# Three quarters of the first layer of the last 1024 tokens by seven products instead of eight, with half of their squares on GpSimd

## Chip, cores and metric

One core of a Trainium2 chip. The time of a run is device microseconds from launch to end. The kernel before was timed three times: median 308.2 us (306.96, 308.2, 310.37). Lower is better.

## The reference

```python
# attention: 8 sequences, 8 heads, 576 positions, 64 wide; window of 32 to either side
scores = scale * q @ k^T;  scores = where(|i - j| <= 32, scores, -1e9)
x = softmax(scores) @ v                    # as 4608 tokens of 512
# two layers behind it: 512 -> 2048 -> 512
h = x @ w_in
r = maximum(h, 0)
out = (s * (r * r) + b) @ w_out
```

Inputs and output are float32; the kernel rounds to bf16 for its products.

## The kernel before

**Attention.** Tokens run through in units of 128 (two tiles of 64 keys). A unit has scores on TensorE (`sc<-qt,kt`, L828), an exponential on ScalarE (L856), a multiplication by a mask on VectorE (L860), the product with V on TensorE (`avn<-vb,ex`, L886) and a division on VectorE (reciprocal L908, `xn` L910). Scores of one unit and the product with V of the unit before are issued together. From the sequence PAIRS = 3 on, q and k come through GpSimd's casts (L780) and transposes by DMA (L796), and the division's result goes by a transposing DMA, issued on SyncE (L934), to `XT`, the activations with features on partitions. `XT` is a ring of 1536 tokens. V is loaded to `VST` and cast to `VB` (L605, L613 and L614).

**First layer.** `s1(m, f0)` (L1135) takes a block of up to 512 tokens and one of 16 groups of 128 features: four matmuls of 128x512 into one of two banks `W` (L1149), Relu on ScalarE into `R1` (L1156; four buffers, each for two feature groups), and once two groups are there, one square over 128x1024 on VectorE into `GT` (L1162). `GT` has two buffers, used in turn by the 512-token groups.

**Second layer.** `second(x)` (L1187) works on 512 tokens. It already uses Winograd's form of Strassen's scheme: seven products instead of eight. Each product is two chains of eight matmuls of 128x256 (L1206), so 14 such groups for 512 tokens. The sums of weights are made once (`weight_sums`, L1173), the sums of activations on VectorE (`total`, L1198: GSUM, and in place in `GT`), and VectorE combines the products with a constant and earlier products in `OUTS` (`combine`, L1222, each reads a bank `O`), which SyncE writes out (L1231). For the last group, `apart`, bank `SC` is used as well and sums S2 and S4 lie in the staging buffers 4 and 5.

**Order.** Every operation is recorded by `add` as a task with its engine, an assumed cost, the buffers that it reads and writes, and a key (the time at which it is wanted). `_Graph.plan` places the tasks one by one: of those whose inputs are there, the one that can start earliest, then the lowest key. Its assumed costs set the order alone. `emit` turns the plan into one fixed list per engine, with semaphore waits where a needed task is on another engine. Each engine then works its list in order: an instruction that waits holds up all behind it. The keys of the layers are in the tables `P1` and `P2` (L431 to L450): in a phase of 512 tokens, 16 groups of the first layer of group x and 14 of the second layer of group x - 1 are interleaved, and the second layer of the last group stands alone at the end. `due` (L471) gives the keys of attention, from the start of the block that reads its tokens.

A flag test (`flag`, L1312) near the end looks whether the exponentials stayed in range; its scratch lies in staging buffers 0 and 1.

Of the kernel before, what the change touches and what calls it, by code (L numbers as in the profile page):

```python
# [9 lines left out]
ALU = mybir.AluOpType  # L10
# [68 lines left out]
class _Graph:  # L79
# [244 lines left out]
def bass_sliding_window_symmetric__then__act_starrelu_kernel(  # L324
# [23 lines left out]
    with ExitStack() as es:  # L348
# [79 lines left out]
        def c1(m):  # L428
            return 4 * (TBLK[m][1] / 2.4 + 2.5) / 1e3
# [4 lines left out]
        for x in range(NG + 1):  # L434
            ms = BLOCKS[x] if x < NG else []
            n2 = 14 if x else 0
            work = sum(16 * c1(m) for m in ms)
            long, start = work + n2 * 0.874, at
            for m in ms:
                PH.append(at)  # L440
                share = long * 16 * c1(m) / work
                for ft in range(16):
                    P1[m, ft] = at + ft / 16.0 * share
                at += share
            for i in range(n2):
                P2[x - 1, i] = start + (i + 0.5) / n2 * long + (DELAY if x < NG else 0.0)
            at = start + long
        PH.append(P2[NG - 1, 0] - 0.5 * n2 / 14 * 0.874)
        PH.append(at)
# [113 lines left out]
        def stg_res(at, n):  # L563
            return [("STG", i) for i in range(at // 64, (at + n) // 64)]
# [251 lines left out]
        def xt_res(t0, t1):  # L816
            return [("XT", x % (XR // 32)) for x in range(t0 // 32, t1 // 32)]
# [306 lines left out]

        def place(m):

            return TBLK[m][0] // 512 % 2, TBLK[m][0] % 512

        def gt_res(gs, fc, c0, n):
            return [("GT", gs, fc, c) for c in range(c0 // 32, (c0 + n) // 32)]  # L1130

        def group(m):
            return 4 if TBLK[m][1] <= 128 else 2 if TBLK[m][1] <= 256 else 1

        def s1(m, f0):  # L1135

            t0, nt = TBLK[m]
            ng = group(m)
            wb = count["w"] % 2
            count["w"] += 1  # L1140
            both = ng == 1
            half = f0 % 2 if both else 0
# [6 lines left out]
            add("pe", [lambda e, g=g, kc=kc: e.matmul(wt[:, g, :],  # L1149
                                                      lhsT=WIN_BF[:, kc, (f0 + g) * 128:(f0 + g + 1) * 128],  # L1150
                                                      rhs=XT[:, kc, t0 % XR:t0 % XR + nt],
                                                      start=(kc == 0), stop=(kc == 3))
                       for g in range(ng) for kc in range(4)],
                1e3 * c1(m) * ng, reads=[("Win", f0 // 4, x) for x in (0, 1)] + xt_res(t0, t0 + nt),
                writes=[("W", wb)], key=key, slack=XTS)
            add("act", lambda e: e.activation(rt, wt, AF.Relu, bias=0.0, scale=1.0),  # L1156
                190 + 0.833 * ng * nt, reads=[("W", wb)], writes=[("R1", rb, half)], key=key)
# [4 lines left out]
            add("dve", lambda e: e.tensor_tensor(GT[gs][:, f1:f1 + nf, g0:g0 + nt], rr, rr, ALU.mult),  # L1162
                130 + 0.55 * nf * nt, reads=[("R1", rb, x) for x in range(2 if both else 1)],
                writes=[r for g in range(nf) for r in gt_res(gs, f1 + g, g0, nt)], key=key)

        def weights_part(y, c0):
            return WOUT_BF.rearrange("p (g y) c -> p g y c", y=2)[:, :, y, c0:c0 + HN]
# [11 lines left out]
                    reads=reads, writes=writes, key=key)  # L1179

        def g_part(x, y, t):
            return GT[x % 2].rearrange("p (g y) c -> p g y c", y=2)[:, :, y, HT * t:HT * t + HT]

        def g_res(x, y, t, halves=(0, 1)):
            return [r for h in halves for g in range(4 * h, 4 * h + 4) for r in gt_res(x % 2, 2 * g + y, HT * t, HT)]

        def second(x):  # L1187

# [54 lines left out]
                s2, s4 = (STG[i].bitcast(BF16).rearrange("p (g c) -> p g c", g=8) for i in (4, 5))  # L1243
                rs2, rs4 = (stg_res(2 * DM * i, 2 * DM) for i in (4, 5))
            for h in (0, 1):
                k = P1[max(BLOCKS[x][-1], NE), 10] if h == 0 else key[0] - 1.0
# [57 lines left out]
        for x in range(1, NG):  # L1304
            for m in BLOCKS[x]:
                attend(m)
                for ft in range(0, 16, group(m)):
                    s1(m, ft)
            second(x - 1)
        second(NG - 1)  # L1310

        def flag():  # L1312

            key = PH[-2] - 24.0
            seen = RECS.rearrange("p u h -> p (u h)")
            low, both = STG[0][:, 0:NU * H], STG[1][:, 0:NU * H]
            low_res, both_res = stg_res(0, 2 * DM), stg_res(2 * DM, 2 * DM)
# [6 lines left out]
            add("pe", lambda e: e.matmul(AVN[:, 0, 0:1], lhsT=ONESW[:, :], rhs=GOOD[:, :], start=True, stop=True), 100,  # L1324
                reads=["ONESW", "GOOD"], writes=[("AVN", 0)], key=key)
# [237 lines left out]
```

## Time and profile before

| what | value |
|---|---|
| median of three runs | 308.2 us |
| the profiled execution, whole | 309.07 us |
| its span, first to last instruction | 307.3 us |
| granted TensorE clock, mean | 1.000 |
| busy: TensorE, VectorE, ScalarE, GpSimd | 95%, 75%, 53%, 21% |
| matmuls of the first layer seen in the trace | 805 |

The profile is one execution. Group lines give line, engine, operation, destination<-sources, shape and count, then busy time in us, mean ns of one, idle time just before and who ended it. Lines in order of time give start and duration in us. PE is TensorE, DVE VectorE, ACT ScalarE, POOL GpSimd, SPq SyncE's queue of DMA issues. The modelled duration of a matmul group reaches into the next one, so the pace is read from start to start. The stretch lines give, for a window, its length and the busy time of PE, PEld (weight loads), DVE, ACT and POOL with the count of instructions, then the granted clock, the DMA share and GB/s.

### The profile page before, as it was taken

To read this page: it belongs to the slowest core of one execution; us is meant where nothing else is said; L and a number is where in the kernel's file an instruction comes from. 1 tells how busy PE (TensorE), PEld (TensorE's weight loads), DVE (VectorE), ACT (ScalarE), POOL (GpSimd) and SP (SyncE) were. 2 spreads that over 40 slices of the span, in tenths; PEclk is the share of its full clock that TensorE was granted. 3 is DMA by queue.
4 is the path that set the end of the run, shared out by engine and by line. 5 is a ranking of instruction groups with operands and counts; after the bars stand their busy time and mean duration, and the time that the engine had idled before them with its cause. 6 is when DMAs were issued, how large, how long until landed. Compare 5 with 4: busy or idle time off the path is not lost.

```text
span 307.3 us, 8802 instructions
## 1 busy us (share of the span) xinstructions
PE 292.1 (95%) x3822; PEld 211.1 (69%) x3849; DVE 230.2 (75%) x394; ACT 164.3 (53%) x261; POOL 63.3 (21%) x77
## 2 busy tenths in 40 slices
PE   8986899999999999999999999999899999999994
PEld 2455778798888887666766675666566666666784
DVE  4665798998769697977699897796876776566673
ACT  3754876695888564757465446543654433333300
POOL 5153568100000242037005400370000000000000
PEclk9999999999999999999999999999999999999999
DMA  6999999999793979999899879897803110200223
GB/s 182 316 265 319 310 288 359 285 246 229 172 194 94 246 136 163 251 236 210 158 286 200 158 178 258 191 184 141 237 17 87 53 47 22 83 30 6 69 70 107
DMA packets 118616, 54.43 MB, mean 177 GB/s; under 512 B 91232, under 2 KB 114400, under 8 KB 118576
## 3 DMA queue, kind: packets, MB, share of 16 engines
q1 hardware_dynamic: 118576, 53.85, 73.4%
q8 instruction: 31, 0.51, 0.7%
q14 instruction: 9, 0.07, 0.1%
HBM read 36.70 MB, written 9.44 MB: 150 GB/s over the span
## 4 chain that ended last, share of the span: by engine, by line
PE 78%; SPq 8%; DMA 5%; DVE 3%; issue 2%; POOL 2%; ACT 1%; POOLq 0%
PE w L1149 35%; PE o L1206 31%; DMA stg<-in_k_dram 4%; PE avn L886 4%; SPq L761 2%; PE sc L1206 2%; PE sc L828 2%; POOL nat L780 2%; SPq L796 1%; DMA vst<-in_v_dram 1%; SPq L650 1%; PE avn L917 1%; SPq L620 1%; SPq L577 1%; DVE kt L699 1%
## 5 line engine op out<-in xcount | busy, mean ns | idle before, releaser
L1149 PE MATMUL w<-xt,win 128*128 128x512 bf16 (+4 forms) x805 | 137.6, 312 | 3.8 <-issue 1.6
L1156 ACT ACTIVATE r<-w 128x512 bf16<-128x512 f32 (+2 forms) x148 | 86.2, 586 | 85.0 <-PE w L1149 82.5
L1149 PEld LDWEIGHTS w<-xt,win 128*128 128x128 bf16 x832 | 73.9, 98 | 34.9 <-ACT r L1156 1.3
L1162 DVE TENSOR_TENSOR gt<-r 128x1024 bf16<-128x1024 bf16 (+3 forms) x100 | 62.3, 629 | 31.4 <-ACT r L1156 30.9
L1206 PE MATMUL o<-wout,gt 128*128 128x256 bf16 x528 | 66.5, 273 | 0.0
L1206 PEld LDWEIGHTS o<-wout,gt 128*128 128x128 bf16 x528 | 50.9, 98 | 13.0
L780 POOL CAST nat<-stg 128x1024 bf16<-128x1024 f32 (+2 forms) x28 | 32.4, 1158 | 80.2 <-DMA stg<-in_q_dram 65.3
L856 ACT ACTIVATE ex<-sc 128x1024 bf16<-128x1024 f32 (+1 forms) x29 | 29.6, 1022 | 17.6 <-PE avn L886 16.3
L1206 PE MATMUL o<-tw,gt 128*128 128x256 bf16 x272 | 34.6, 273 | 0.0
L1222 DVE SCALAR_TENSOR_TENSOR outs<-o,sb,cvec 128x512 f32<-128x512 f32 (+1 forms) x36 | 25.7, 715 | 8.2 <-PE o L1206 7.9
L1206 PEld LDWEIGHTS o<-tw,gt 128*128 128x128 bf16 x272 | 26.3, 98 | 7.4
L1222 DVE SCALAR_TENSOR_TENSOR outs<-o,sb,outs 128x512 f32<-128x512 f32 (+1 forms) x27 | 19.3, 715 | 8.4 <-PE o L1206 8.3
L1198 DVE TENSOR_TENSOR gt<-gt 128x1024 bf16<-128x1024 bf16 (+1 forms) x26 | 23.7, 913 | 0.2
L860 DVE TENSOR_TENSOR ex<-ex,mask 128x1024 bf16<-128x1024 bf16 (+1 forms) x29 | 21.5, 740 | 1.4 <-ACT ex L856 0.9
L910 DVE TENSOR_TENSOR xn<-avn,rec 128x512 bf16<-128x512 f32 (+1 forms) x31 | 21.2, 685 | 0.5
L886 PE MATMUL avn<-vb,ex 64*64 64x65 bf16 x944 | 19.9, 197 | 0.3
L886 PEld LDWEIGHTS avn<-vb,ex 64*64 64x64 bf16 x944 | 12.9, 107 | 9.1 <-issue 4.7
L1206 PE MATMUL o<-tw,gsum 128*128 128x256 bf16 x136 | 17.6, 273 | 0.0
L1206 PEld LDWEIGHTS o<-tw,gsum 128*128 128x128 bf16 x136 | 13.1, 98 | 3.9
L1198 DVE TENSOR_TENSOR gsum<-gt 128x1024 bf16<-128x1024 bf16 x18 | 13.0, 721 | 0.4
L925 ACT COPY xt<-avn 128x512 bf16<-128x512 bf16 (+2 forms) x18 | 9.4, 531 | 4.9 <-PE avn L917 4.9
L828 PE MATMUL sc<-qt,kt 64*64 64x128 bf16 x440 | 11.7, 216 | 0.0
(132 smaller groups left out, 232.1 us busy)
## 6 DMA issues: line engine op xcount, KB each, us to landing
out_dram<-outs SPq DMA_DIRECT2D x32, 256.0 KB, 3.0
vst<-in_v_dram SPq DMA_DIRECT2D x28, 256.0 KB, 4.2
stg<-in_k_dram SPq DMA_DIRECT2D x24, 256.0 KB, 6.4
stg<-in_q_dram SPq DMA_DIRECT2D x5, 1024.0 KB, 6.5
stg<-in_moe_w_in_dram SPq DMA_DIRECT2D x8, 512.0 KB, 7.4
stg<-in_moe_w_out_dram SPq DMA_DIRECT2D x8, 512.0 KB, 7.3
stg<-in_q_dram SPq DMA_DIRECT2D x4, 512.0 KB, 8.9
stg<-in_k_dram SPq DMA_DIRECT2D x4, 512.0 KB, 8.9
```

The costliest lines, as they stand in the source:

```text
L780: (lambda e, dst=dst, src=src: e.tensor_copy(dst, src)),
L828: fns = [lambda e, pr=pr, x=x, b=b, j=j, hp=hp: e.matmul(SC[64 * x:64 * x + 64, hp, pr * 128:pr * 128 + 128], lhsT=k_tile(b, pr, j)[64 * h ...
L856: add("act", lambda e, dst=flat_dst, src=flat_src: e.activation(dst, src, AF.Exp, bias=0.0, scale=0.125), 190 + 0.833 * 512 * len(hs), rea ...
L860: add("dve", lambda e, flat=flat, mask=mask: e.tensor_tensor(flat, flat, mask, ALU.mult), 130 + 0.53 * 512 * len(hs), reads=[("E", ei, hp, ...
L886: return [lambda e: e.matmul(av[64 * x:64 * x + 64, h, 0:D + 1], lhsT=buf[64 * g:64 * g + 64, h % 2, h // 2, c:c + 64], rhs=VB[64 * g:64 * ...
L910: add("dve", lambda e: e.tensor_tensor(XN[xi][0:p1, :].rearrange("p (a c) -> p a c", a=H), av[0:p1, :, 0:D], REC[ri][0:p1, :].rearrange("p ...
L1149: add("pe", [lambda e, g=g, kc=kc: e.matmul(wt[:, g, :], lhsT=WIN_BF[:, kc, (f0 + g) * 128:(f0 + g + 1) * 128], rhs=XT[:, kc, t0 % XR:t0 % ...
L1156: add("act", lambda e: e.activation(rt, wt, AF.Relu, bias=0.0, scale=1.0), 190 + 0.833 * ng * nt, reads=[("W", wb)], writes=[("R1", rb, ha ...
L1162: add("dve", lambda e: e.tensor_tensor(GT[gs][:, f1:f1 + nf, g0:g0 + nt], rr, rr, ALU.mult), 130 + 0.55 * nf * nt, reads=[("R1", rb, x) fo ...
L1198: add("dve", lambda e: e.tensor_tensor(dst, x, y, op), 1240.0 if half is None else 690.0, reads=reads, writes=writes, key=k)
L1206: add("pe", [lambda e, g=g, j=j, dst=dst: e.matmul(dst, lhsT=lhs[:, g, 128 * j:128 * j + 128], rhs=rhs[:, g, :], start=first and g == 0 an ...
L1222: add("dve", lambda e, src=src, dst=dst, other=other: e.scalar_tensor_tensor(dst, src, SB128[:, 0:1], other, ALU.mult, ALU.add), 200 + 1.0 ...
```

## The change

The last two groups of 512 tokens (t = 0, 1) now share the first layer of 12 of the 16 feature groups. Two feature groups and two token groups make a quad; there are six. With A the weights (A11, A12: the first feature group, upper and lower half of the 512 inputs; A21, A22: the second) and B the activations, a quad takes seven products of two matmuls of 128x512 each, in place of eight such products (sixteen matmuls).

- **Weight sums** S1 to S4 on GpSimd (`SUMS`): for the first four quads over 128x1024 into `NAT` 0 to 3, for the last two over 128x512 into the exponentials' buffers. **Token differences** T1 to T4 on VectorE over 128x1024 into `VST` 0 to 3.
- **A quad's chain** (`quad_group`): bank `AVN` or `SC`, in turn, which attention needs no more. Half 0 of the bank gathers products 1, 6, 7 and 4 one after the other; after 1, 6 and 7 ScalarE keeps a copy of the running sum in float32 (`keep`). Half 1 gathers products 5 and 3; product 2 goes to a bank `W`. Three joins on VectorE add a bank and a kept sum into `R1`; the fourth output is left in half 0 and rectified from there. Each following product of a chain waits for the copy, or the join, of the one before.
- **Rectify** on ScalarE: 512, 1024 and 512 columns. **Squares** over 128x1024: those of the last token group on GpSimd, those of the one before on VectorE (`TURNS`).
- The last group's `GT` becomes the staging buffers 0 to 3 (`home`, `gt_res`); the kept sums lie in staging buffers 4 and 5 and `NAT` 4 and 5. The flag's scratch moves to `VST` 4.
- **Keys.** All six quads stand in the phase of the last group but one, behind the four feature groups that are left of it; the last phase has four feature groups. Attention of the last 1024 tokens is due earlier (`due`). The key of the first half of the last group's sums in `second` is that of feature group 3 instead of 10.

```diff
+QUADS = 6
+FASTEST = 16 - 2 * QUADS
+TRAIL = 2.0
+FIN = 0.75
+LEAD = 7.0
+TURNS = ("pool", "dve") * QUADS
+HELD = 4
+SUMS = ("pool", "pool")
...
-            work = sum(16 * c1(m) for m in ms)
+            fts = range(FASTEST) if x == NG - 1 else range(16)
+            quads = 28 * c1(NM - 1) / 4 * QUADS if x == NG - 2 else 0.0
+            work = sum((FASTEST if x >= NG - 2 else 16) * c1(m) for m in ms) + quads
...
+            if blk >= NM - 2:
+                return PH[NM - 3] - LEAD + (tok - TBLK[NM - 2][0]) / 1024 * (P1[NM - 2, FASTEST] - PH[NM - 3])
...
+        def home(x):
+            return 2 if x == NG - 1 else x % 2
+
+        GTS = GT + [STGS[:, 0:4096].bitcast(BF16).rearrange("p (f c) -> p f c", f=16)]
...
+        def quad_sums():
...
+                for dst, a, b, op, reads, i in ((S1, a21, a22, ALU.add, [], 0), (S2, S1, a11, ALU.subtract, own[0], 1),
+                                                (S3, a11, a21, ALU.subtract, [], 2), (S4, a12, S2, ALU.subtract, own[1], 3)):
+                    eng = SUMS[part]
+                    add(eng, lambda e, dst=dst, a=a, b=b, op=op: e.tensor_tensor(dst, a, b, op),
+                        510.0 * n if eng == "pool" else 140.0 + 141.0 * n,
+                        reads=Win + reads, writes=own[i], key=P1[NM - 2, ft] - (20.0 if part == 0 else 6.0) + 0.1 * i)
...
+            for dst, a, b, reads, i in ((T1, B12, B11, early + late_, 0), (T2, B22, T1, late_ + [("VST", 0)], 1),
+                                        (T3, B22, B12, late_, 2), (T4, B21, T2, early + [("VST", 1)], 3)):
+                add("dve", lambda e, dst=dst, a=a, b=b: e.tensor_tensor(dst, a, b, ALU.subtract), 700.0,
+                    reads=reads, writes=[("VST", i)], key=key - 2.0 + 0.1 * i)
...
+        def quad_group(i):
...
+            product(1, chain, True, key[0])
+            keep(p1, p1r, key[0])
+            product(2, other, True, key[1])
+            product(6, chain, False, key[2])
+            keep(u2, u2r, key[2])
+            join(other, p1, p1r, ra, 0, key[1])
+            product(5, side, True, key[3])
+            product(7, chain, False, key[4])
+            keep(u3, u3r, key[4])
+            join(side, u3, u3r, rb, 1, key[4])
+            product(3, side, False, key[5])
+            join(side, u2, u2r, rb, 0, key[5])
+            product(4, chain, False, key[6])
+            rectify(A[:, 0:512], A[:, 0:512], [("R1", ra, 0)], ra, (0,), key[3])
+            rectify(C[:, :], C[:, :], [("R1", rb, x) for x in (0, 1)], rb, (0, 1), key[6])
+            rectify(A[:, 512:1024], chain[1], [chain[0]], ra, (1,), key[6])
+            square(rb, 1, TURNS[2 * i], key[7])
+            square(ra, 0, TURNS[2 * i + 1], key[7])
...
-                for ft in range(0, 16, group(m)):
+                for ft in range(0, 16 if x < NG - 2 else FASTEST, group(m)):
                     s1(m, ft)
+            if x == NG - 2:
+                attend(NM - 1)
+                quad_sums()
+                for i in range(QUADS):
+                    quad_group(i)
             second(x - 1)
```

More of the change, by code (lines that the diff above doesn't have):

```diff
@@ L440, in bass_sliding_window_symmetric__then__act_starrelu_kernel @@
                 PH.append(at)
-                share = long * 16 * c1(m) / work
-                for ft in range(16):
-                    P1[m, ft] = at + ft / 16.0 * share
+                share = long * ((FASTEST if x >= NG - 2 else 16) * c1(m) + quads) / work
+                for ft in fts:
+                    P1[m, ft] = at + ft / len(fts) * share * (FIN if x == NG - 1 else 1.0)
+                    if quads:
+                        P1[m, ft] = at + (ft * c1(m) if ft < FASTEST else FASTEST * c1(m) + (ft - FASTEST) / (16 - FASTEST) * quads) * long / work
+                        P1[m + 1, ft] = P1[m, ft] + 0.05
                 at += share
             for i in range(n2):
-                P2[x - 1, i] = start + (i + 0.5) / n2 * long + (DELAY if x < NG else 0.0)
+                P2[x - 1, i] = start + (i + 0.5) / n2 * long + (TRAIL if x == NG - 2 else DELAY if x < NG else 0.0)
             at = start + long
@@ L1125, in place @@
         def place(m):
-            return TBLK[m][0] // 512 % 2, TBLK[m][0] % 512
+            return home(TBLK[m][0] // 512), TBLK[m][0] % 512
+        def home(x):
+            return 2 if x == NG - 1 else x % 2
+        GTS = GT + [STGS[:, 0:4096].bitcast(BF16).rearrange("p (f c) -> p f c", f=16)]
         def gt_res(gs, fc, c0, n):
+            if gs == 2:
+                return [("STG", 4 * fc + c) for c in range(c0 // 128, (c0 + n - 1) // 128 + 1)]
             return [("GT", gs, fc, c) for c in range(c0 // 32, (c0 + n) // 32)]
@@ new lines, in quad_group, with product, keep, join @@
+        def quad_group(i):
+            f0, z = FASTEST + 2 * i, i % 2
+            m = NM - 2
+            name, bank = (("AVN", AVN), ("SC", SC))[z]
+            wb = count["w"] % 2
+            count["w"] += 1
+            ra, rb = count["r"] % NR1, (count["r"] + 1) % NR1
+            count["r"] += 2
+            chain, side, other = ((name, 0), bank[:, 0, :]), ((name, 1), bank[:, 1, :]), (("W", wb), W[:, wb, :])
+            key = [P1[m, f0] + (P1[m, f0 + 1] - P1[m, f0]) * x / 3.5 for x in range(8)]
+            parts = [(stg_res(2 * DM * 4 + 512 * x, 512), STG[4 + x // 2][:, 512 * (x % 2):512 * (x % 2) + 512]) for x in range(4)] + \
+                [([("NAT", x)], NAT[x].bitcast(F32)) for x in (4, 5)]
+            (p1r, p1), (u2r, u2), (u3r, u3) = parts[3 * z:3 * z + 3]
+            def product(n, dst, first, k):
+                (lhs, lres), (rhs, rres) = weight[i // HELD][n], quad[n]
+                add("pe", [lambda e, kk=kk: e.matmul(dst[1], lhsT=lhs(i % HELD, kk), rhs=rhs[:, kk, :], start=first and kk == 0, stop=(kk == 1),
+                                                     skip_group_check=True) for kk in (0, 1)],
+                    c1(m) * 500.0, reads=lres + rres, writes=[dst[0]], key=k, slack=XTS if n < 3 else 0.0)
+            def keep(dst, res, k):
+                add("act", lambda e: e.copy(dst, chain[1]), 617.0, reads=[chain[0]], writes=res, key=k)
+            def join(src, mine, res, r, half, k):
+                add("dve", lambda e: e.tensor_tensor(R1[r][:, 512 * half:512 * half + 512], src[1], mine, ALU.add), 660.0,
+                    reads=[src[0]] + res, writes=[("R1", r, half)], key=k)
+            def rectify(dst, src, reads, r, halves, k):
+                add("act", lambda e: e.activation(dst, src, AF.Relu, bias=0.0, scale=1.0), 190 + 0.833 * 512 * len(halves),
+                    reads=reads, writes=[("R1", r, x) for x in halves], key=k)
+            def square(r, t, eng, k):
+                gs = home(NG - 2 + t)
+                rr = R1[r][:, :].rearrange("p (g c) -> p g c", g=2)
+                add(eng, lambda e: e.tensor_tensor(GTS[gs][:, f0:f0 + 2, :], rr, rr, ALU.mult), 700.0 if eng == "dve" else 2100.0,
+                    reads=[("R1", r, x) for x in (0, 1)], writes=[x for g in (0, 1) for x in gt_res(gs, f0 + g, 0, 512)], key=k)
+            A, C = R1[ra], R1[rb]
+            product(1, chain, True, key[0])
[16 more added lines that the diff above has]
+            square(ra, 0, TURNS[2 * i + 1], key[7])
@@ L1181, in g_part @@
         def g_part(x, y, t):
[L1182 removed]
+            return GTS[home(x)].rearrange("p (g y) c -> p g y c", y=2)[:, :, y, HT * t:HT * t + HT]
         def g_res(x, y, t, halves=(0, 1)):
[L1185 removed]
+            return [r for h in halves for g in range(4 * h, 4 * h + 4) for r in gt_res(home(x), 2 * g + y, HT * t, HT)]
         def second(x):
```

35 lines of the change are left out of this document (31 added, 4 removed).

## The prediction

> **What bounds the kernel now.** I read the page's busy line, then busy time by stretch for the last third, TensorE's waits there, the order of single instructions, and last the groups by shape.
>
> ```profile
> PE 292.1 (95%) x3822; PEld 211.1 (69%) x3849; DVE 230.2 (75%) x394; ACT 164.3 (53%) x261; POOL 63.3 (21%) x77
> ```
> ```profile
> 240.00:260.00 20.00, 19.72 (x154) 12.99 (x155) 13.75 (x22) 7.19 (x13) 0.00 (x0) 1.00 0.14 39
> 260.00:280.00 20.00, 19.84 (x137) 13.33 (x138) 11.36 (x16) 7.17 (x13) 0.00 (x0) 1.00 0.16 53
> ```
> ```profile
> PE w L1149 <- ACT r L1156: 1.2, 2, 1.0
> ```
>
> The second column of the stretches is TensorE: 95% busy overall, over 98% from 240 us on, at granted clock 1.00 (the last but two). VectorE (fourth) has a third of that time free, ScalarE almost two thirds, GpSimd all. The third fence is the one kind of wait for another engine that TensorE has after 200 us, 1.2 us in all. So a matmul removed there shortens the run, and whatever makes TensorE wait lengthens it. The pace:
>
> ```profile
> 246.75 1.04 PE L1206 MATMUL o<-wout,gt 128*128 128x256 bf16 x8
> 247.62 1.03 PE L1149 MATMUL w<-xt,win 128*128 128x512 bf16 x4
> ...
> 250.22 1.04 PE L1206 MATMUL o<-wout,gt 128*128 128x256 bf16 x8
> ```
>
> Four groups start within 250.22 - 246.75 = 3.47 us: 0.868 us for a group of either layer, 0.217 us for one 128x512 matmul.
>
> **The matmuls.** For the features concerned, two 512-token blocks took 2 x 12 x 4 = 96 matmuls of 128x512; six quads of seven products of two take 84. Twelve fewer: 12 x 0.217 = **-2.60 us**, if TensorE stays fed. Second layer and attention keep their matmuls; they only move.
>
> **A stall that goes.** Before, ScalarE's cast of V stood ahead of a rectify and waited for a load that was issued behind four transposes:
>
> ```profile
> 211.05 0.58 SPq L605 DMA_DIRECT2D vst<-in_v_dram  x1
> ...
> 214.91 0.62 ACT L613 CAST vb<-vst 128x512 bf16<-128x512 f32 x1 [2.35 <-DMA vst<-in_v_dram]
> 215.43 1.08 ACT L1156 ACTIVATE r<-w 128x512 bf16<-128x512 f32 x2
> ...
> 216.07 1.04 PE L1149 MATMUL w<-xt,win 128*128 128x512 bf16 x4 [1.05 <-ACT r L1156]
> ```
>
> In the changed order on SyncE that load stands ahead of those transposes, and ScalarE's next one is issued about 212.3; landing 3.8 us later, as this one did, it meets its cast about on time. So **-1.05 us**, ends -1.05 and 0. The transposes to XT issued some 1.8 us later on SyncE instead are first read some 25 us of matmuls further on: zero.
>
> **Work given to the other engines.** Durations:
>
> ```profile
> L1162 DVE TENSOR_TENSOR gt<-r 128x1024 bf16<-128x1024 bf16 x26 | 18.8, 722 | 16.4 <-ACT r L1156 16.2
> L1222 DVE SCALAR_TENSOR_TENSOR outs<-o,sb,cvec 128x512 f32<-128x512 f32 x13 | 9.7, 745 | 3.5 <-PE o L1206 3.5
> ...
> L1198 DVE TENSOR_TENSOR gsum<-gt 128x1024 bf16<-128x1024 bf16 x7 | 4.8, 687 | 0.1
> L910 DVE TENSOR_TENSOR xn<-avn,rec 128x512 bf16<-128x512 f32 x6 | 4.1, 690 | 0.2
> ...
> L1198 DVE TENSOR_TENSOR gt<-gsum,gt 128x2048 bf16<-128x2048 bf16 x3 | 3.6, 1215 | 0.0
> ```
> ```profile
> L1156 ACT ACTIVATE r<-w 128x512 bf16<-128x512 f32 x105 | 62.6, 597 | 74.1 <-PE w L1149 72.1 <-PE avn L1324 1.1 <-DVE ex L860 0.8
> L856 ACT ACTIVATE ex<-sc 128x1024 bf16<-128x1024 f32 x21 | 21.5, 1023 | 16.1 <-PE avn L886 15.7
> ```
> ```profile
> L580 POOL CAST win<-stg 128x1024 bf16<-128x1024 f32 x8 | 8.5, 1065 | 10.8 <-PE avn L634 5.8 <-DMA stg<-in_moe_w_in_dram 5.1
> ```
>
> Per quad ScalarE gets three keeps and two short rectifies of 0.60 and a long one of 1.02 us: 4.0 us. VectorE gets three joins (one operand in PSUM; the nearest row is xn, 0.69) and one square; GpSimd one square. From the first token difference to VectorE's last square of a quad, TensorE has 84 matmuls, 14 groups of the second layer and 6 of the first: 18.2 + 12.2 + 5.2 = 35.6 us. VectorE has 18 joins, 8 squares, 4 token differences and 4 half totals of 0.69, 2 whole totals of 1.2 and 8 combines of 0.745: 23.5 + 2.4 + 6.0 = 31.9 us. ScalarE has 6 x 4.0 and 6 rectifies, 27.6 us. Both fit, VectorE with 3.7 us to spare.
>
> No row shows GpSimd with two inputs. Its cast, one input, is 1.07 us, the lower end; two casts drawn out as in the next rows, 2.9, are the upper. I take 2.1, the cast twice, one for each read.
>
> **What GpSimd and VectorE do to each other** decides the rest. GpSimd's casts, then VectorE in the same microseconds:
>
> ```profile
> 167.66 2.81 POOL L780 CAST nat<-stg 128x1024 bf16<-128x1024 f32 x2
> ```
> ```profile
> 170.54 2.40 POOL L780 CAST nat<-stg 16x1024 bf16<-16x1024 f32 x2
> ```
> ```profile
> 168.06 0.68 DVE L910 TENSOR_TENSOR xn<-avn,rec 128x512 bf16<-128x512 f32 x1
> ...
> 169.51 1.52 DVE L860 TENSOR_TENSOR ex<-ex,mask 128x1024 bf16<-128x1024 bf16 x1
> 170.95 1.52 DVE L1162 TENSOR_TENSOR gt<-r 128x1024 bf16<-128x1024 bf16 x1
> ```
>
> The mask and the square, both inputs in SBUF, take 1.52 us instead of 0.69, the casts 1.40 instead of 1.07, in turns; xn, with one operand in PSUM, keeps its 0.68. So joins and combines go free, and masks, squares, differences and totals wait for a running GpSimd instruction: 0.83 us behind a cast of 1.07, all but 0.24 of it; behind one of 2.1, some 1.9. The Trainium skill ("SBUF — State Buffer", section Who interferes with whom) says that a VectorE instruction with two SBUF inputs contends with a GpSimd instruction that reads SBUF, and that the loser blocks for the whole instruction; the 1.52 us agree. Were the port shared by bandwidth, both would only slow down by a part, and the sum below would come near 305.
>
> *Weight sums, first part.* Four of GpSimd's sums and differences over 128x1024 stand behind its last casts. One may run early; three wait for the last transposes of that sequence:
>
> ```profile
> 209.77 1.24 SPq L796 DMA_TRANSPOSE kt<-nat  x1
> ```
> ```profile
> kt<-nat SPq DMA_TRANSPOSE x2, 3.5
> ```
> ```profile
> 217.91 0.32 PE L886 MATMUL avn<-vb,ex 64*64 64x65 bf16 x16
> ```
>
> They run from 209.77 + 3.5 = 213.3 us, back to back. In the changed order VectorE then has a whole total, a square and the mask for the attention unit that stood at 217.91 (now 217.7: 1.05 less of stall, one group of 0.87 more ahead). In turns: sum to 215.4, total 216.6, sum 218.5, square 219.1, sum 221.0, mask 221.7; TensorE waits 4.0 us. If VectorE gets the port twice running, the mask ends near 219.7, a wait of 2. If the sums fall beside PSUM work, 0. I take **+2.0**, the middle of the ends. The second part, four of half the width beside the last attention unit, delays one square by about 1 us; TensorE needs nothing of it within 2: +0.1.
>
> *Squares on GpSimd.* I walked two quads through the new order with these durations and the delays in the rows:
>
> ```profile
> 302.41 1.04 PE L1206 MATMUL sc<-tw,gt 128*128 128x256 bf16 x8
> ...
> 303.49 0.48 DVE L1222 SCALAR_TENSOR_TENSOR outs<-sc,sb,cvec 128x256 f32<-128x256 f32 x1 [0.39 <-PE sc L1206]
> ```
>
> (302.41 + 0.87 to 303.49: 0.21 from TensorE to a reader; and under 0.1 from the first rectify of 215.43 to the matmuls of 216.07.) One step of a chain is product 0.43, delay 0.21, keep 0.60, delay 0.08 = 1.3 us. Two quads take 14 products and 5 groups, 10.4 us, each with four such steps, so a step has 2.6. I found every product's operands ready, the nearest (quad 2's second kept sum, before its seventh product) 0.7 us early. GpSimd's squares hold VectorE up by 0.3 to 0.9 us there, which its idle time takes. Not at the end: VectorE's last square meets GpSimd's square of the quad before and comes 0.5 us late, and TensorE's next second layer waits for it: **+0.5**. Behind it a half total and GpSimd's last square want the port together. If GpSimd wins, the totals up to the one that the third product needs come 2 us late, of which TensorE sees 1.6; if not, 0. I take half, **+0.8**.
>
> *Start and end.* Attention's last units come some 10 us of matmuls earlier, at closest 3.35 us apart; from scores over exponential and mask to the next product is 0.21 + 1.02 + 0.08 + 0.69 + 0.08 = 2.1 of the 2.6 us between them: zero. The token differences wait on VectorE for the last transposes to XT; 2.7 us of other VectorE work stands in front, and before the change such a transpose landed 2.4 us after its issue:
>
> ```profile
> xt<-xn SPq DMA_TRANSPOSE x4, 2.4
> ```
>
> Zero here too; a landing 2 us later costs up to 1.5. After the last matmul the same combine and store follow: zero. The last block's totals now come beside the last products: 12 of 0.69, 2 of 1.2, 7 combines of 0.745 and 14 of 0.48, 22.6 us under 27 of matmuls; a bank freed late could cost 0.8, which I leave to the range.
>
> **Sum.** -2.60 - 1.05 + 2.0 + 0.1 + 0.5 + 0.8 = -0.25 us on the profiled execution's 309.07 (span 307.3 and 1.77 around it): 308.8. That execution lies 0.87 above the median of the runs, 308.2; on the median the result is **308.0 us**. The Trainium skill ("GPSIMD Engine Reference", section Performance versus the Vector engine) gives 4497 ns for a two-input instruction over 2048 elements, so an estimated 2.25 us for 1024; no row here shows one, and the sum would be 308.3 by it.
>
> **Rivals.** *GpSimd stays out of the way.* Sums and squares fall where VectorE reads PSUM: for it speaks that the casts after 200 us cost TensorE no wait for VectorE (third fence); against it the 1.52 us. Then 308.2 - 3.65 = 304.6, to 306.1 with the last square. *VectorE becomes the bound of the quads, and the kernel slower.* It has 3.7 us to spare, so from a mean hold of 3.7 / 6 = 0.6 us per GpSimd square on it sets the time. At 1.2 it is 6 x 1.2 - 3.7 = 3.5 us more, 311.5; at the full 1.9, 7.7 more, 315.7. For it: joins stand in order behind held squares, chains behind joins. Against: one GpSimd square in 5 us, rarely met for its full length. *Late transposes* alone: +1.5, 309.5. That the matmuls are not saved is no rival: the order has 84 for 96.
>
> **How the numbers follow.** About 1% is what a measurement of this kernel can tell from no change: 305.1 and 311.3 are its bounds. The forecast case gets 0.53 (0.01 below 305.1, 0.03 above 311.3), GpSimd out of the way 0.22 (0.11 below), VectorE as the bound 0.20 (0.12 above), late transposes 0.05 (0.01 above). Faster 0.12, same 0.72, slower 0.16. The range runs from 304.9, inside the first rival, to 312.2, inside the second, and leaves out some 0.18; the likeliest case alone spans 307.2 (last square unopposed) to 310.8 (sums in turns, last square late).
>
> **What would show it.** 84 matmuls in the new products; GpSimd rows of about 2.1 us for 128x1024 (above 2.6 the slow rival gains); squares, masks or totals of 2 us or more on VectorE beside GpSimd's sums between 213 and 222 us, and TensorE waiting about 2 us for a mask near 218; no ScalarE wait of 2 us for vst near 214; a wait of about 1 us at the first group after the last quad. Waits spread over all quads would mean that VectorE or the chains are the bound, no waits at all the fast rival; either proves the forecast wrong.

## The result: 4.7 us slower, and where the time went

The changed kernel takes 311.78 us (median of 14 runs, 309.15 to 313.32), the kernel before 307.08 (14 runs, 304.16 to 310.59): a ratio of 1.016, 95% interval 1.013 to 1.019. Forecast was 308.0 us, no change that can be measured. 311.8 lies inside the range given, 304.9 to 312.2, but the kernel is clearly slower. The profiled execution took 312.37 us (span 310.6, mean clock 0.989).

The busy line of the page, changed kernel:

```profile
PE 291.1 (94%) x3809; PEld 210.8 (68%) x3837; DVE 247.0 (80%) x410; ACT 171.9 (55%) x273; POOL 90.9 (29%) x91
```

TensorE is busy for 1.0 us less than before, in a span 3.3 us longer: the time is waiting, and, as the clock column below shows, matmuls that run slower. TensorE's waits after 195 us (in all, times, longest) say for whom it waits:

```profile
PE avn L901 <- DVE ex L875: 4.4, 1, 4.4
PE o L1333 <- DVE gt L1325: 0.9, 1, 0.9
...
PE o L1333 <- DVE outs L1349: 0.2, 1, 0.2
```

One wait of 4.4 us for a masked exponential stands out. Busy time by stretch (length, then TensorE, weight loads, VectorE, ScalarE, GpSimd with counts, granted clock, DMA share, GB/s), changed kernel:

```profile
210.00:220.00 10.00, 6.36 (x82) 3.64 (x80) 8.77 (x6) 4.40 (x7) 9.44 (x4) 0.98 0.77 192
220.00:230.00 10.00, 8.90 (x130) 5.91 (x133) 7.67 (x13) 3.24 (x4) 0.23 (x1) 0.68 0.15 41
240.00:260.00 20.00, 19.68 (x136) 12.34 (x131) 18.87 (x28) 9.99 (x18) 4.75 (x4) 1.00 0.15 45
260.00:280.00 20.00, 19.89 (x125) 12.16 (x126) 15.62 (x25) 15.38 (x25) 8.17 (x5) 1.00 0.10 34
```

and the first two stretches of the kernel before:

```profile
210.00:220.00 10.00, 8.68 (x147) 5.80 (x147) 6.92 (x12) 4.96 (x8) 0.00 (x0) 1.00 0.79 190
220.00:230.00 10.00, 9.95 (x111) 6.49 (x110) 7.41 (x13) 4.80 (x9) 0.00 (x0) 1.00 0.24 59
```

From 240 to 280 us, where the six quads lie, TensorE is as full as before. Most of the loss stands in two neighbouring stretches: from 210 to 220 us TensorE is 2.3 us less busy, and from 220 to 230 us the clock column has 0.68 in place of 1.00. VectorE and GpSimd in the first of them, in order of time:

```profile
212.79 2.93 DVE L1325 TENSOR_TENSOR gt<-gsum,gt 128x2048 bf16<-128x2048 bf16 x1
215.65 2.60 DVE L1184 TENSOR_TENSOR gt<-r 128x1024 bf16<-128x1024 bf16 x1
218.18 2.60 DVE L875 TENSOR_TENSOR ex<-ex,mask 128x1024 bf16<-128x1024 bf16 x1
```
```profile
210.33 4.32 POOL L1215 TENSOR_TENSOR nat<-win 128x1024 bf16<-128x1024 bf16 x2 [4.69 <-DMA kt<-nat]
214.73 2.98 POOL L1215 TENSOR_TENSOR nat<-nat,win 128x1024 bf16<-128x1024 bf16 x1
217.78 2.44 POOL L1215 TENSOR_TENSOR nat<-win,nat 128x1024 bf16<-128x1024 bf16 x1
```

The two lists interleave strictly. The first total starts at 212.79, inside GpSimd's second sum, which ends at 210.33 + 4.32 = 214.65; the total takes 2.93 = 1.86 of waiting and some 1.1 of work, and ends at 215.72. The third sum, started at 214.73, waits for that and takes 2.98 where the first two took 4.32 together. VectorE's square waits for the third sum (2.60 in place of 0.69), the fourth sum for the square, the mask for the fourth sum (2.60 again). The mask is through at 220.78, and the product that needs it starts:

```profile
214.52 1.89 PE L1171 MATMUL w<-xt,win 128*128 128x512 bf16 x8
220.83 0.43 PE L901 MATMUL avn<-vb,ex 64*64 64x65 bf16 x16 [4.41 <-DVE ex L875]
...
223.95 1.49 PE L1171 MATMUL w<-xt,win 128*128 128x512 bf16 x3 [0.22 <-issue]
225.23 1.59 PE L1333 MATMUL o<-wout,gt 128*128 128x256 bf16 x8
226.65 1.02 PE L1171 MATMUL w<-xt,win 128*128 128x512 bf16 x4
```

After the idle stretch each group of matmuls also takes longer: three of the first layer 1.49 us, eight of the second 1.59, against 0.81 and 1.04 at full clock. That is the 0.68 of the clock column; by 226.65 four take 1.02, as ever.

The other places that the prediction named. The quads, the pace from start to start:

```profile
262.52 1.04 PE L1333 MATMUL o<-tw,gsum 128*128 128x256 bf16 x8
263.39 1.03 PE L1252 MATMUL sc<-vst,nat 128*128 128x512 bf16 x4
264.25 1.04 PE L1333 MATMUL o<-tw,gt 128*128 128x256 bf16 x8
```

A group takes 0.87 us as before; the trace has 83 records for the 84 matmuls of the new products. And the end of the quads, on GpSimd, VectorE and TensorE:

```profile
277.78 1.89 POOL L1270 TENSOR_TENSOR stg<-r 128x1024 bf16<-128x1024 bf16 x1 [2.82 <-ACT r L1264]
280.64 2.05 POOL L1270 TENSOR_TENSOR stg<-r 128x1024 bf16<-128x1024 bf16 x1 [0.97 <-ACT r L1264]
```
```profile
279.39 0.82 DVE L1270 TENSOR_TENSOR gt<-r 128x1024 bf16<-128x1024 bf16 x1
...
280.98 2.27 DVE L1325 TENSOR_TENSOR gt<-gt 128x1024 bf16<-128x1024 bf16 x1
```
```profile
285.70 1.92 PE L1333 MATMUL o<-wout,gt 128*128 128x256 bf16 x16 [0.87 <-DVE gt L1325]
```

The last square of VectorE is hardly touched (0.82). The half total at 280.98 waits for GpSimd's last square, 2.27 in place of 0.69, and TensorE then waits 0.87.

### The profile page after: what moved, and what is told of

It reads as the page before. It is cut to its first block, busy times and chain, and to the rows that moved or that the text cites. A ratio compares the mean times of both kernels' runs of the same rounds, so it can differ in the third digit from the quotient of the medians.

```text
span 310.6 us, 8846 instructions
## 1 busy us (share of the span) xinstructions
PE 291.1 (94%) x3809; PEld 210.8 (68%) x3837; DVE 247.0 (80%) x410; ACT 171.9 (55%) x273; POOL 90.9 (29%) x91
## 4 chain that ended last, share of the span: by engine, by line
PE 77%; DMA 8%; DVE 6%; SPq 4%; issue 3%; POOL 1%; DVEq 0%; POOLq 0%
PE o L1333 32%; PE w L1171 27%; DMA stg<-in_moe_w_in_dram 5%; PE avn L901 4%; DMA stg<-in_k_dram 3%; PE sc L1252 2%; PE avn L1252 2%; PE sc L843 2%; PE sc L1333 2%; SPq L592 2%; SPq L665 1%; SPq L635 1%; PE avn L932 1%; DVE outs L1349 1%; DVE gt L1184 1%
## 5 line engine op out<-in xcount | busy, mean ns | idle before, releaser
L1171 PE MATMUL w<-xt,win 128*128 128x256 bf16 (+4 forms) x712 | 114.8, 304 | 2.7 <-issue 1.8
L1178 ACT ACTIVATE r<-w 128x512 bf16<-128x512 f32 (+2 forms) x124 | 71.8, 584 | 65.8 <-PE w L1171 64.5
L1171 PEld LDWEIGHTS w<-xt,win 128*128 128x128 bf16 x736 | 64.9, 98 | 27.7 <-issue 1.5
L1184 DVE TENSOR_TENSOR gt<-r 128x512 bf16<-128x512 bf16 (+3 forms) x86 | 54.4, 642 | 19.9 <-ACT r L1178 19.8
L1333 PEld LDWEIGHTS o<-wout,gt 128*128 128x128 bf16 x512 | 49.6, 99 | 14.1 <-DVE gt L1325 1.4
L1333 PE MATMUL o<-tw,gt 128*128 128x256 bf16 x256 | 32.2, 273 | 0.0
L1333 PEld LDWEIGHTS o<-tw,gt 128*128 128x128 bf16 x256 | 24.7, 98 | 6.5
L875 DVE TENSOR_TENSOR ex<-ex,mask 128x1024 bf16<-128x1024 bf16 (+1 forms) x29 | 23.6, 813 | 1.5 <-ACT ex L871 0.9
L1270 POOL TENSOR_TENSOR stg<-r 128x1024 bf16<-128x1024 bf16 x6 | 11.5, 1919 | 27.3 <-ACT r L1264 27.3
L595 POOL CAST win<-stg 128x1024 bf16<-128x1024 f32 x8 | 9.3, 1161 | 13.1 <-DMA stg<-in_moe_w_in_dram 13.1
```

Source lines behind the costliest of these rows:

```text
L875: add("dve", lambda e, flat=flat, mask=mask: e.tensor_tensor(flat, flat, mask, ALU.mult), 130 + 0.53 * 512 * len(hs), reads=[("E", ei, hp, ...
L1171: add("pe", [lambda e, g=g, kc=kc: e.matmul(wt[:, g, :], lhsT=WIN_BF[:, kc, (f0 + g) * 128:(f0 + g + 1) * 128], rhs=XT[:, kc, t0 % XR:t0 % ...
L1184: add("dve", lambda e: e.tensor_tensor(GTS[gs][:, f1:f1 + nf, g0:g0 + nt], rr, rr, ALU.mult), 130 + 0.55 * nf * nt, reads=[("R1", rb, x) f ...
L1333: add("pe", [lambda e, g=g, j=j, dst=dst: e.matmul(dst, lhsT=lhs[:, g, 128 * j:128 * j + 128], rhs=rhs[:, g, :], start=first and g == 0 an ...
```

## The experiments

Theory A: GpSimd's four weight sums, each reading two operands, take turns with VectorE's totals, squares and masks; the mask comes 4.4 us late, and the idle stretch lowers TensorE's clock behind it. Rival B: the squares on GpSimd (or the quads' chains) cost the time, and the wait at 220 us would be there without the sums, because of the other order. Ratios are to the kernel before on the same chip, with 95% intervals.

**The first four sums on VectorE.**

```diff
-SUMS = ("pool", "pool")
+SUMS = ("dve", "pool")
```

> The first four weight sums (128x1024) go from GpSimd to VectorE; all else as in the changed kernel. Theory A (GpSimd's sums hold the SBUF port against VectorE, the mask comes late, TensorE waits 4.4 us and then runs 2.4 us at a lower clock): the wait for the mask near 217 us and the slow stretch after it are gone, the granted clock is 1.00 there, and the time falls by about 6.5 us from the changed kernel, to a ratio of 0.99 to 1.00 against the kernel before. Theory B (the loss lies in the quads and the last phase, through squares on GpSimd and chains through ScalarE): at most 2 us of it, a ratio of 1.010 or more.

Measured: 0.9945 [0.9908, 0.9983], clock 1.00 in every stretch of 10 us from 210 to 300 us. TensorE's waits after 195 us, without a last one of 0.2 for a combine:

```profile
PE avn L901 <- DMA kt<-nat: 0.9, 1, 0.9
PE o L1333 <- DVE gt L1325: 0.9, 1, 0.9
```

The 4.4 us are gone with the sums, and with them the lower clock. This edit also moves the order on VectorE, so the next leaves all lists alone.

**The same sums on GpSimd, each held back behind an attention product.**

```diff
                         reads=Win + reads, writes=own[i], key=P1[NM - 2, ft] - (20.0 if part == 0 else 6.0) + 0.1 * i,
+                        waits=[land["av", LONG, 18 + i]] if part == 0 else [])
```

> The first four weight sums stay on GpSimd, but each waits for the attention product of one more unit, so that they run one per unit instead of back to back; every engine's order is that of the changed kernel. Theory A: one sum at a time delays a VectorE instruction by at most 1.9 us, which the mask's slack of about 2 us covers; no wait of 4 us, clock 1.00, ratio 0.99 to 1.00. If it is GpSimd's work as such and not its crowding that costs, the waits stay, spread over four units, about 1 us each, ratio about 1.01. Theory B: 1.010 or more.

Measured: 1.005 [1.0015, 1.0086], between the two kernels. Its waits, and VectorE's rows where a sum ran:

```profile
PE avn L901 <- DVE ex L875: 1.9, 3, 1.3
PE o L1334 <- DVE gt L1326: 0.9, 1, 0.9
PE o L1334 <- DVE outs L1350: 0.7, 1, 0.7
```
```profile
216.95 2.60 DVE L1184 TENSOR_TENSOR gt<-r 128x1024 bf16<-128x1024 bf16 x1
...
221.93 2.09 DVE L629 CAST vb<-vst 128x512 bf16<-128x512 f32 x1
...
226.75 2.24 DVE L1326 TENSOR_TENSOR gsum<-gt 128x1024 bf16<-128x1024 bf16 x1
```

A sum that has VectorE to meet only once delays one instruction by 1.5 to 1.9 us (the square 2.60 in place of 0.69, a half total 2.24 in place of 0.69) instead of a row of them. The four together still leave TensorE 1.9 us of waits for masks, in three pieces, and 0.7 for a combine. So theory A's mechanism holds, and its expectation of no cost was wrong: VectorE has no time to spare from 220 to 230 us, where it is busy for 9.97 of the 10.

**All squares on VectorE, the sums as changed.**

```diff
-TURNS = ("pool", "dve") * QUADS
+TURNS = ("dve", "dve") * QUADS
```

> All squares of the quads on VectorE, the weight sums on GpSimd as in the changed kernel. Theory A: the wait of 4.4 us for the mask and the slow clock behind it stay; only the wait of 0.9 us at the end of the quads goes, if VectorE's longer list does not bring another; ratio 1.010 to 1.018. Theory B (squares on GpSimd are the loss): ratio 1.000 or below.

Measured: 1.0193 [1.0141, 1.0244]; the 4.5 us stay, and the wait of 0.9 at the end of the quads falls to 0.2:

```profile
PE avn L901 <- DVE ex L875: 4.5, 1, 4.5
PE avn L901 <- DMA kt<-nat: 1.0, 1, 1.0
```

Rival B's first half falls: without any square on GpSimd the kernel is no faster.

**The kernel before, with the four sums added and nothing else** (their results aren't used).

```diff
             second(x - 1)
+            if x == NG - 2:
+                attend(NM - 1)
...
+                for dst, a, b_, op, reads, i in ((S1, a21, a22, ALU.add, [], 0), (S2, S1, a11, ALU.subtract, [("NAT", 0)], 1),
+                                                (S3, a11, a21, ALU.subtract, [], 2), (S4, a12, S2, ALU.subtract, [("NAT", 1)], 3)):
+                    add("pool", lambda e, dst=dst, a=a, b_=b_, op=op: e.tensor_tensor(dst, a, b_, op), 2040.0,
```

> The kernel before, with the four weight sums of 128x1024 added on GpSimd at the place where the changed kernel has them; their results are not used, and every other engine's order is unchanged. Theory A: total, square and mask on VectorE between 213 and 221 us take 2 us or more each, TensorE waits 2.5 to 4 us for the mask and runs at a lower clock for a few us behind it: 3 to 6 us more, ratio 1.010 to 1.020. Theory B: GpSimd is idle there in the kernel before, so nothing: 1.000.

Measured: 1.0211 [1.0156, 1.0265]. The wait appears in the kernel before:

```profile
PE avn L886 <- DVE ex L860: 3.1, 1, 3.1
PE w L1149 <- ACT r L1156: 1.2, 1, 1.2
```
```profile
220.00:230.00 10.00, 9.72 (x153) 6.66 (x154) 8.57 (x16) 5.16 (x8) 0.00 (x0) 1.00 0.21 54
```

The second half of rival B falls too: the old order has the same wait once the sums are there. In this trace 3.1 us of idle time left the clock at 1.00. That execution took 311.48 us; the other five took 311.12 to 314.3 at mean clocks of 0.983 to 0.995, which would fit a clock lowered in them, but the quickest of all, 311.12, is among these with 0.991, and no trace of them was seen.

**The kernel before, with eight memsets on GpSimd in the same place**, of 128x1024 each, which read nothing.

```diff
+            if x == NG - 2:
+                attend(NM - 1)
+                for i in range(8):
+                    add("pool", lambda e, i=i: e.memset(NAT[i // 2][:, :], 0.0), 1020.0, writes=[("NAT", i // 2)], key=P1[NM - 2, 4] - 20.0 + 0.1 * i)
```

> The kernel before, with eight memsets of 128x1024 on GpSimd (writes into the same buffers, nothing read) in place of the four sums of the run before this one, about 8 us of GpSimd work at the same place; orders unchanged, results not used. If GpSimd's reads are what VectorE waits for (theory A), masks, squares and totals keep 0.69 and 1.2 us and the ratio is 1.000. If any GpSimd work beside VectorE costs, they lengthen as beside the sums, and the ratio is 1.010 or more.

Measured: 1.0025 [0.9981, 1.0068]. GpSimd, and VectorE's total and mask within the same microseconds:

```profile
207.85 8.17 POOL L1312 MEMSET nat<- 128x1024 bf16 x8 [3.32 <-DMA kt<-nat]
```
```profile
210.25 1.22 DVE L1198 TENSOR_TENSOR gt<-gsum,gt 128x2048 bf16<-128x2048 bf16 x1
...
213.98 0.68 DVE L860 TENSOR_TENSOR ex<-ex,mask 128x1024 bf16<-128x1024 bf16 x1
```

As long a stretch of GpSimd work, and VectorE keeps its 1.22 and 0.68 (a cast of V beside it takes 0.55 in place of 0.42): it isn't GpSimd at work that delays VectorE, it is GpSimd reading. The Trainium skill ("SBUF — State Buffer", section Who interferes with whom) says the same of instructions that only write; this run agrees.

**The idle time filled with matmuls.** To see the price of the clock apart from the wait, unused matmuls were put directly ahead of the waiting product, first 18.

```diff
+            if ripe == (LONG, 18):
+                busy.append(add("pe", [lambda e: e.matmul(AVN[:, 0, :], lhsT=ONESW[:, :], rhs=ONESW[:, :].rearrange("p (one c) -> p one c", one=1)
+                                                          .to_broadcast((128, 4, 128)), start=True, stop=True) for _ in range(18)],
+                                1.0, reads=["ONESW"], writes=[("AVN", 0)], key=due(*ripe)))
...
+        g.order.remove(busy[0])
+        g.order.insert(g.order.index(land["av", LONG, 18]), busy[0])
```

> The changed kernel with 18 extra matmuls of 128x512 on constants, without use, put on TensorE directly ahead of the attention product that waits for the mask; they run inside the wait (18 x 0.217 = 3.9 us of 4.4). All other orders are unchanged. If the idle time lowered the clock, the granted clock stays at 1.00 from 220 to 230 us and the time falls by about 2.4 us from the changed kernel although TensorE does more: ratio 1.006 to 1.010. If the lower clock has another cause, the ratio stays at 1.016.

Measured: 1.0121 [1.007, 1.0172], more than the 1.006 to 1.010 expected, with the mask as late as before and a wait of 0.6 us left. Since that interval meets the changed kernel's, three kernels were then run on one chip: 6 matmuls, none, and 18.

> The kernel of the kept-busy run with 6 unused 128x512 matmuls instead of 18 ahead of the waiting AV product (4.05 us for 18 there, so 1.35 us for 6); nothing else differs and the output is unaffected. Its question is how long an idle stretch of TensorE may be before the granted clock falls. Theory A (a stretch over some bound between 3.1 us, where the kernel before with sums kept 1.00, and 4.4 us, where the changed kernel fell to 0.68, lowers the clock once): the wait left over is 4.4 - 1.35 = 3.05 us, the clock of 220 to 230 us stays 1.00, and the time is that of the 18 matmuls, 0.4 to 1 per cent under the changed kernel. Rival B (the clock falls in proportion to the idle time): the clock of that stretch lies near 0.8 and the time halfway between the two.

> The changed kernel as it stands, on the same chip as the runs with 6 and with 18 matmuls, so that the price of the lower clock comes from one chip. Theory A (4.4 us of wait and some 2 us of lower clock): ratio 1.014 to 1.019, a wait of 4.2 to 4.6 us, clock of 220 to 230 us between 0.6 and 0.85. Rival (the lower clock costs nothing that the end sees): the ratio equals that of the 18 matmuls within 0.3 per cent.

> The kept-busy kernel (18 unused matmuls in the wait) again, in more rounds and beside the changed kernel. Theory A: clock 1.00 throughout, and 1 to 2.5 us (0.3 to 0.8 per cent) under the changed kernel, still 0.8 to 1.2 per cent over the kernel before, since VectorE delivers the masked exponentials as late as in the changed kernel. Rival (the clock costs nothing): within 0.3 per cent of the changed kernel.

Measured: 6 matmuls 1.0099 [1.0059, 1.0138]; none 1.0118 [1.0073, 1.0163]; 18 matmuls 1.0086 [1.0049, 1.0123]. The changed kernel is here below the 1.014 to 1.019 that was expected, and the times don't tell the three apart. The profiles do. The 6 matmuls (a wait of 3.2 us), by waits and stretch; then none, by stretch and order; then 18 in the same way:

```profile
PE avn L901 <- DVE ex L875: 3.2, 1, 3.2
```
```profile
220.00:230.00 10.00, 9.43 (x195) 6.84 (x199) 9.26 (x18) 5.17 (x7) 0.00 (x0) 1.00 0.21 54
```
```profile
220.00:230.00 10.00, 9.32 (x186) 6.73 (x188) 8.15 (x15) 3.84 (x5) 0.00 (x0) 0.83 0.22 54
```
```profile
220.49 0.43 PE L901 MATMUL avn<-vb,ex 64*64 64x65 bf16 x16 [4.51 <-DVE ex L875]
...
225.05 1.03 PE L1171 MATMUL w<-xt,win 128*128 128x512 bf16 x4
```
```profile
220.00:230.00 10.00, 9.74 (x183) 6.94 (x175) 9.25 (x18) 5.39 (x7) 0.00 (x0) 1.00 0.23 56
```
```profile
219.64 0.32 PE L901 MATMUL avn<-vb,ex 64*64 64x65 bf16 x16 [0.64 <-DVE ex L875]
...
222.91 1.03 PE L1175 MATMUL w<-xt,win 128*128 128x512 bf16 x4
```

After 3.2 us of idle time the clock of the next stretch is 1.00, after 4.5 us 0.83, after the 4.41 us of the first profile 0.68. From the late product to the same four first-layer matmuls, 18 matmuls take 222.91 - 219.64 = 3.27 us, the changed kernel 225.05 - 220.49 = 4.56 here and 226.65 - 220.83 = 5.82 in the first profile. The lower clock thus costs 1.3 to 2.55 us in these traces. The mean clocks of the runs without a trace can be read by these, with caution: a stretch of 10 us at 0.83 lacks 1.7 us of a span of 309, which makes a mean of 0.994; 0.68, with the 0.98 before it, lacks 3.4 and makes 0.989. The 14 runs of the changed kernel have 0.983 to 0.994, 13 of the 17 with 18 matmuls 0.999 or 1.0. With 6 matmuls three of 12 have 1.0, nine 0.989 to 0.995. A mean alone doesn't show where the clock fell: the kernel before, on the chip of these runs, has 0.992 to 0.994 in 5 of 22. But the means of the changed kernel go with its times: its six runs at 0.993 or 0.994 have a median of 310.0 us, its eight at 0.983 to 0.989 one of 311.9.

So filling the wait does away with the lower clock in the traces, and in most runs by their means. The bound that theory A supposed above 3.1 us is not confirmed: the traced run with 3.2 us kept 1.00, and the means of the others make it likely, though not shown, that 3.2 us lower the clock too. That the means of the changed kernel and of the 6 matmuls come in steps of about 0.0055 also speaks against rival B's proportion.

**Two versions without the delays.** First sums and the last quad's square on VectorE; and no GpSimd at all in the change.

```diff
-TURNS = ("pool", "dve") * QUADS
+TURNS = ("pool", "dve") * (QUADS - 1) + ("dve", "dve")
-SUMS = ("pool", "pool")
+SUMS = ("dve", "pool")
```
```diff
-TURNS = ("pool", "dve") * QUADS
+TURNS = ("dve", "dve") * QUADS
-SUMS = ("pool", "pool")
+SUMS = ("dve", "dve")
```

> First weight sums on VectorE, and the last quad's square on VectorE instead of GpSimd; the other five squares stay on GpSimd. By theory A both new waits go (4.4 and 0.9 us) and the lower clock with them: 7 us under the changed kernel, ratio 0.985 to 0.993 against the kernel before. If the last square only changes places in VectorE's list, the 0.9 us stay: 0.990 to 0.996.

> All sums and all squares of the change on VectorE, nothing new on GpSimd: the seven products alone. VectorE then has 31.9 + 6 x 0.69 = 36 us in the 35.6 us of the quads. By theory A no wait for a mask; if VectorE becomes the bound, waits of 1 to 3 us in all, spread over the quads, and a ratio of 0.995 to 1.003; if its list still fits, 0.985 to 0.993.

Measured: 0.9938 [0.9907, 0.9969] and 0.9935 [0.9889, 0.9982], both just above the 0.985 to 0.993 of theory A. Waits of the first, then of the second:

```profile
PE avn L901 <- DMA kt<-nat: 1.0, 1, 1.0
...
PE o L1333 <- DVE outs L1349: 0.2, 1, 0.2
```
```profile
PE o L1333 <- DVE gt L1270: 0.8, 1, 0.8
PE o L1333 <- DVE outs L1349: 0.4, 1, 0.4
```

Both are faster than the kernel before and than the changed one, and neither can be told from the run with only the first sums moved (0.9945). So the change as a whole is worth some 2 us (0.65%, interval 0.2 to 1.1) with VectorE doing everything, and GpSimd's squares bring nothing and cost nothing that shows. Moving the last square removes the wait of 0.87 for the total, but the time doesn't show it.

## Why the prediction was wrong

**Wrong: the first four weight sums, "+2.0, the middle of the ends".** The working named the place, both engines and the order in turns, and put the mask at 221.7 with a wait of 4.0 for it. It was 220.78 and 4.41. The delay of one meeting, "some 1.9", was right as well (the square: 2.60 less 0.69), and so was the order of the last three sums; all four ran back to back from 210.33, where the working let one run early and the others start at 213.3. What failed is the choice: the middle of 0 and 4 was taken although the rows of 167 to 172 us already showed the two engines in strict turns (1.52, 1.40), and none showed VectorE getting through twice running. The ends were not equally likely, so the middle had no row behind it. Moving these four sums alone turned 1.016 into 0.9945. But with the upper end, 4.0, the sum would have given 310.0, still no change that can be told; the other half of the miss is the next term.

**Missing: the clock behind the wait.** The sum priced a wait at its own length. A wait of this length also slowed the matmuls after it, 2.55 us in the first profile and 1.3 in the second; the prediction had nothing for it. The longest wait of TensorE in the last third of the kernel before is 1.05 us, so it could have been given only as a page's rule: the Trainium skill ("TensorE: Matmul & The Clock Gate", section What's actually happening) says that the clock is halved after an idle window of 3.4 us, and that these windows run freely. By that rule one window at half clock takes 1.7 us out of a stretch of 10, which leaves 0.83, and two leave 0.66 (an estimate from the page's figures); measured were 0.83 and 0.68, and 1.00 after 3.2 us, so the traces agree. The runs without a trace are another matter: by that rule a stretch shorter than the window leaves the clock alone, while nine of the 12 runs with 6 matmuls have a lower mean, and how long their waits were isn't known.

**Right: -2.60 for twelve matmuls.** Their pace stayed 0.87 us for four, and nothing waits in the quads. No run measures this term by itself.

**Mostly right: -1.05 for the stall.** No trace of the changed kernel has TensorE wait for that rectify. But ScalarE still waits for the load of V ahead of it, where the working had it land about on time: 1.05 us in the first profile (2.35 before), up to 2.1 in others.

```profile
215.50 0.62 ACT L628 CAST vb<-vst 64x512 bf16<-64x512 f32 x1 [1.05 <-DMA vst<-in_v_dram]
```

And a new wait can come up, of TensorE for transposes of k: 0.9 us where the first sums are on VectorE, 1.0 with the last square there too and 1.0 with all squares but not the sums there, 0.2 to 0.6 in the second profile of the changed kernel and in the runs with sums held back or matmuls added, nothing in the first profile and without GpSimd. That the attention of the last 1024 tokens is asked for earlier may be the reason; no run tested it, and the kernel before with the sums added has 0.3 as well. The working gave the transposes to XT and the last units their due, and not these.

**The two gains together.** With the waits that their profiles show, the terms leave -3.65 + 1.03 + 0.15 = -2.5 us for the version with the last square on VectorE and -3.65 + 0.79 + 0.42 = -2.4 for the one without GpSimd. The ratios give -1.9 and -2.0, and their intervals hold both.

**The end of the quads.** "+0.8", half of 1.6: measured 0.87, but by luck: GpSimd's square did come first, for which the working had 1.6, and TensorE saw only half of that. "+0.5" for the last square: no wait, as GpSimd's square ran only 0.28 us into it (277.78 + 1.89 less 279.39). The second sums, "+0.1": 0.16 at a combine, a wait that is gone without GpSimd. Quads, late transposes to XT, start and end: no wait, as worked out.

With the measured terms: -2.60 - 1.05 + 4.41 + 2.55 + 0.2 + 0.87 = +4.4 us, against 4.7 between the medians. The two profiled executions differ by only 3.3, as the one of the kernel before had lost some 0.9 more by 200 us. The group of the second layer that starts at 201.82 us there starts at 199.99 in the changed kernel, which has one attention unit more still to come (0.97 us, from 197.50 + 0.87 to 199.34). From that group to the end it takes 310.6 - 199.99 - 0.97 = 109.6 us, against 307.3 - 201.82 = 105.5: 4.2 more. Of the 4.9 us between the forecast change, -0.25, and the 4.7, the wait's length accounts for 2.4 and the clock for 2.55; the rest nearly cancels.

**The rivals.** VectorE as the bound of the quads had the right sign and the wrong place: the quads have no wait, and GpSimd's squares of 1.9 us mostly found VectorE idle or at joins and combines, which kept their 0.68 and 0.75 us (at 259.49 and 258.82, beside the square at 258.71); the one VectorE square that was much drawn out took 1.31, at 269.43. "GpSimd stays out of the way" is excluded by three rows of 2.6 us and more. The range reached 312.2 for that slower rival and so held 311.8 by a mechanism that didn't occur; the chance of 0.16 for slower had the case that came, sums in turns, priced only up to 310.8. That the time lay inside the range was luck. (The 306.1 of the first rival has no working: 304.6 with the 0.5 and 0.8 of the last square is 305.9.)

## What to carry to other kernels

Where the trace shows two engines taking strict turns, walk the order in turns and take that end, not the middle: a queue of sums on the idle engine hands its length on to every instruction of the busy one, so four sums of 2.1 us came out as one wait of 4.4. Before moving work to GpSimd, ask whether it reads on-chip memory in the microseconds in which VectorE works on two operands that something waits for; memsets, and squares that mostly met VectorE idle or reading PSUM, cost nothing that could be measured here. Price a wait of this length above its length: in the traces 4.4 to 4.5 us of idle time were followed by a lower clock that cost 1.3 to 2.55 us more.

## What the runs showed of the hardware

- A GpSimd instruction over two operands of 128x1024 took 2.12 us where it had begun before VectorE's instruction (the run with the sums held back), as the prediction had it, 2.1; with one operand read twice (the squares) 1.89. In turns with VectorE it took 2.44 to 2.98, and VectorE's 0.69 became 2.60.
- VectorE's cast of V to bf16, which has one operand, also waited for a GpSimd sum: 2.09 us at 221.93 in the run with the sums held back, 0.42 alone. The prediction had let only instructions with two operands in on-chip memory wait, although the kernel before shows such a cast with 1.26 us at 160.78 and 1.25 at 204.59, beside GpSimd's casts.
- Eight GpSimd memsets, 8.17 us, left VectorE's totals, squares and masks at 1.22 and 0.69 us.
- A clock of 0.68 to 0.83 over 10 us after one idle stretch of 4.4 to 4.5 us, and 1.00 in the traces with 3.2 and 3.1; by the means of the other runs it is likely, not shown, that 3.2 us lower it too.
